# A recurrent-memory and linear-attention kernel on one core: a wider margin for waits on transfers, a new order of all work, and four spinning groups of other tile shapes

## The chip, the core and the metric

The kernel runs on one core of one Trainium2 chip. The time is the device time of that core in microseconds, from one launch of the whole program. A run of it was profiled; the rows of its trace are quoted below as "the profile". Names of the engines in it: PE is TensorE (matmuls), PEld its weight loads, DVE is VectorE, ACT ScalarE, POOL GpSimd, SP SyncE. A `q` behind an engine's name is its instruction queue, which issues transfers.

## What is computed

Two layers of two blocks each over x of 2048 tokens by 512. Block A is an attention with 32 heads of 128 that goes through the tokens in 64 segments of 32, and carries 8 memory rows from one segment to the next, so the segments form one chain. Block B is a linear attention over all tokens with 32 heads of 16.

```python
def A(x, mem0, Wq, Wk, Wv, Wo):
    mem = mem0
    for s in range(64):
        h = concat([mem, x[:, 32*s:32*s+32]], axis=1)        # 8 + 32 rows
        q, k, v = h @ Wq, h @ Wk, h @ Wv                     # 32 heads of 128
        p = softmax(where(mask, q @ k.T * scale, -1e9))
        o = (p @ v) @ Wo
        mem = o[:, :8]
        outs.append(o[:, 8:])
    return concat(outs, axis=1)

def B(x, wqkv, wo):
    pq, pk = phi(q), phi(k)                                  # phi(t) = (t + 1 if t > 0 else exp(t)) + 1e-6
    num, den = pq @ (pk.T @ v), pq @ sum(pk)
    return (num / (den + 1e-6)) @ wo

x = x + A(layernorm(x), ...)
x = x + B(layernorm(x), ...)
x = x + A(layernorm(x), ...)
x = x + B(layernorm(x), ...)
```

## The kernel before

All four large weight matrices are loaded once and stay in SBUF. Tokens are held in 16 tiles of 128 rows; a tile has four segments. A segment is projected to k and q (`kq0`, `kq1`: two halves of the heads) and to v (`v`), each in matmuls that use the PE array as four column groups of 32 (`tile_position`). The results come from PSUM through ScalarE or VectorE (L2009 and L2010, the two branches of one helper `copy`), and are brought into head order by 32x32 transposes of VectorE (L2301). Then, in `mem_attention`, the scores (L2443 for keys of the other groups' tokens, L2435 for the rest), two exponentials on ScalarE, and the new memory rows (L2471); `out_block` (L2563) and `next_mem` (L2593) close the chain to the next segment. `x_attention` (L2501 to L2545) does the same for the segment's 32 tokens, a little later.

The output rows of a segment, in `y_sb`, are brought to their token rows in `dx_sb` by small transfers: `rows_out` issues one 24-row move each on GpSimd's queue (semaphore `dy0`) and on SP's queue (`dz0`) per segment, and for each tile four 8-row moves on either queue (`dy1`, `dz1`). When a tile is complete, one VectorE instruction (L2642) adds `dx_sb` to the tile in `x_sb`. It is the only reader of `dx_sb`. `prepare` normalises the next tile and turns it with a transposing transfer on SP's queue (L2180); `b_in` does block B's first pass over the finished tile, and `b_out` its second pass. Between the layers, `late_queries` does the queries that block B's first pass left out, and GpSimd's queue stores them in DRAM scratch (`pq_scratch`).

No scheduler runs on the chip or in the build. Each piece of work is a node. The table `PLACE` at the top of the file holds one planned number (in ns) for each node, under the key (layer, step, name); a trailing `a` or `v` puts it on ScalarE or VectorE where both can do it. `schedule` sorts all nodes by these numbers; an engine executes its own nodes in that order. `BANKS` gives each PSUM tile its bank. `finalize` (L1765) finds which semaphores a node must wait for, beyond what its engine knows already. A node of ScalarE, VectorE or TensorE with more than one wait keeps the wait whose source is planned last; the others may be put on an earlier node of the same engine, among the last 40, that has no wait yet and is planned later than the source. For a transfer the source's time is taken from the one transfer whose count on the semaphore is the awaited one, as its planned issue plus its planned latency plus a margin (L1808). Several transfers of a group may share a semaphore, and then the wait is over only when all that count towards the value have landed.

At the start, while the weights arrive, TensorE executes groups of matmuls of ones whose results nobody reads (`spin`; L2167 and, without a new weight load, L2139): eleven groups in `first_left_blocks` ahead of the first projections, and six more behind them.

## Time and profile before

| | us |
|---|---|
| three runs: median (lowest to highest) | 1473.34 (1466.6 to 1479.05) |
| the profiled execution, its own time | 1474.65 |
| its span in the trace, first to last instruction | 1472.8 |
| mean granted TensorE clock | 0.997 of full speed |

The page of the profile gives each engine's busy time, the chain of work that ended last, and the costliest groups. Rows of waits read: who waited, for what, the total in us, how often, the longest. Rows of the timeline read: start, length in us, engine, line, what is written and read, count, and in brackets how long the engine had been idle and what ended that. A matmul counts as busy until its result is there, and several overlap; so TensorE can be busy while it does less than it could.

### The profile page before, as it was taken

The numbers are of one execution on the slowest core, as the hardware profiler recorded it, in microseconds if no ns is written. First come the engines' busy times: TensorE is split into PE (matmuls) and PEld (weight loads), VectorE is DVE, ScalarE is ACT, GpSimd is POOL, SyncE is SP. The second block draws the span as 40 slices with busy tenths as digits, with TensorE's granted clock in tenths as the row PEclk, the third lists the DMA queues.
The fourth block names the chain that finished last, engine by engine and source line by source line (L and its number), as shares of the span: only waits on it lengthen the run. The fifth ranks groups of instructions, "written<-read, shape, count | busy, mean of one in ns | idle before, by whom it ended". The sixth has DMA issues, their size and how long they took to land.

```text
span 1472.8 us, 90913 instructions
## 1 busy us (share of the span) xinstructions
PE 1434.8 (97%) x43673; PEld 839.5 (57%) x39641; DVE 1244.9 (85%) x3928; ACT 897.7 (61%) x2532; POOL 205.6 (14%) x407
## 2 busy tenths in 40 slices
PE   9999999999999999999899999999999999999988
PEld 5555555555555555656455555555555565666554
DVE  5888878898887888878888888888888888888878
ACT  3556555656656666665566566556666666666557
POOL 3111111011110101111200110111111111111010
PEclk9999999999999999999999999999999999999999
DMA  9411111111100101112210010111011111101034
GB/s 385 178 50 40 31 29 46 25 26 21 25 25 10 26 20 29 26 22 49 67 25 14 25 29 24 28 26 29 20 23 27 25 28 26 29 14 27 29 65 128
DMA packets 84968, 65.14 MB, mean 44 GB/s; under 512 B 65544, under 2 KB 76360, under 8 KB 83048
## 3 DMA queue, kind: packets, MB, share of 16 engines
q1 hardware_dynamic: 70584, 40.21, 10.2%
q0 software_dynamic: 13840, 18.98, 4.7%
q8 instruction: 326, 5.34, 1.6%
q14 instruction: 58, 0.48, 0.1%
q10 hardware_dynamic: 160, 0.14, 0.0%
HBM read 27.80 MB, written 14.02 MB: 28 GB/s over the span
## 4 chain that ended last, share of the span: by engine, by line
PE 86%; DVE 5%; DMA 5%; ACT 1%; SPq 1%; issue 1%; POOL 1%; DVEq 0%
PE pb L2282 39%; PE pb L2563 18%; PE pb L2139 13%; PE pb L2151 3%; PE pb L2513 3%; DMA dx_sb<-y_sb 2%; PE pb L2755 2%; PE pb L2471 2%; PE pb L2533 2%; PE pb L2435 2%; PE pb L2593 1%; DMA arena_sb<-arena_sb 1%; DVE arena_sb L2488 1%; DMA x_sb<-in_A_x_dram 1%; SPq L2026 1%
## 5 line engine op out<-in xcount | busy, mean ns | idle before, releaser
L2009 ACT ACTIVATE arena_sb<-pb 128x512 bf16<-128x512 f32 (+3 forms) x1013 | 501.4, 524 | 257.5 <-PE pb L2139 108.2
L2282 PE MATMUL pb<-Wk_sb,arena_sb 128*32 128x512 bf16 x4320 | 358.6, 380 | 0.9 <-DVE arena_sb L2010 0.7
L2282 PE MATMUL pb<-Wv_sb,arena_sb 128*32 128x512 bf16 x4608 | 332.6, 380 | 0.0
L2563 PE MATMUL pb<-Wo_sb,arena_sb 128*32 128x256 bf16 x10368 | 323.9, 273 | 0.9 <-DVE arena_sb L2545 0.3
L2301 DVE STREAM_TRANSPOSE arena_sb<-arena_sb 128x256 f32<-128x256 f32 x640 | 259.7, 427 | 35.4 <-ACT arena_sb L2009 25.7
L2563 PEld LDWEIGHTS pb<-Wo_sb,arena_sb 128*32 128x32 bf16 x10368 | 263.9, 97 | 38.8 <-DVE arena_sb L2478 11.7
L2026 POOL DMA_DIRECT2D dx_sb<-y_sb x246 | 125.2, 513 | 997.6 <-DVE y_sb L2575 459.3
L2282 PE MATMUL pb<-Wq_sb,arena_sb 128*32 128x512 bf16 x3088 | 238.0, 380 | 1.1 <-DVE arena_sb L2010 1.1
L2282 PEld LDWEIGHTS pb<-Wk_sb,arena_sb 128*32 128x32 bf16 x4320 | 122.8, 96 | 176.0 <-issue 87.4
L2139 PE MATMUL pb<-Wq_sb,arena_sb 128*32 128x512 bf16 x2032 | 201.4, 379 | 0.0
L2486 ACT ACTIVATE arena_sb<-pb,arena_sb 128x128 bf16<-128x128 f32 x469 | 142.9, 369 | 72.5 <-DVE arena_sb L2540 22.7
L2488 DVE TENSOR_TENSOR arena_sb<-pb,arena_sb 128x128 bf16<-128x128 f32 (+2 forms) x422 | 171.3, 406 | 11.5 <-DMA dx_sb<-y_sb 1.7
L2282 PEld LDWEIGHTS pb<-Wv_sb,arena_sb 128*32 128x32 bf16 x4608 | 114.6, 95 | 70.8 <-issue 7.1
L2010 DVE CAST arena_sb<-pb 128x512 bf16<-128x512 f32 (+2 forms) x248 | 127.4, 516 | 30.9 <-PE pb L2282 8.3
L2009 ACT ACTIVATE outW_sb<-pb 128x256 f32<-128x256 f32 (+1 forms) x132 | 50.7, 384 | 144.0 <-PE pb L2563 96.8
L2282 PEld LDWEIGHTS pb<-Wq_sb,arena_sb 128*32 128x32 bf16 x3088 | 86.0, 97 | 88.1 <-issue 26.3
L2513 PE MATMUL pb<-arena_sb 128*32 128x130 bf16 x3072 | 106.7, 219 | 0.2
L2523 DVE STREAM_TRANSPOSE arena_sb<-arena_sb 128x192 f32<-128x192 f32 x256 | 93.4, 365 | 15.1 <-ACT arena_sb L2486 6.6
L2501 DVE TENSOR_TENSOR arena_sb<-arena_sb,wx_sb 128x1280 bf16<-128x1280 bf16 x128 | 102.1, 797 | 1.2 <-ACT arena_sb L2454 0.8
L2471 PEld LDWEIGHTS pb<-arena_sb 128*32 128x32 bf16 x2016 | 45.5, 96 | 72.0 <-ACT arena_sb L2009 33.9
L2513 PEld LDWEIGHTS pb<-arena_sb 128*32 128x32 bf16 x3072 | 69.2, 96 | 29.8 <-issue 6.5
L2575 DVE TENSOR_TENSOR y_sb<-pb,outW_sb 64x256 bf16<-64x256 f32 x162 | 68.8, 424 | 18.7 <-ACT outW_sb L2009 14.3
(135 smaller groups left out, 1830.2 us busy)
## 6 DMA issues: line engine op xcount, KB each, us to landing
Wk_sb<-in_A_Wk_dram SPq DMA_DIRECT2D x4, 1024.0 KB, 9.6
Wq_sb<-in_A_Wq_dram SPq DMA_DIRECT2D x4, 1024.0 KB, 17.9
Wv_sb<-in_A_Wv_dram SPq DMA_DIRECT2D x4, 1024.0 KB, 25.4
Wo_sb<-in_A_Wo_dram SPq DMA_DIRECT2D x8, 512.0 KB, 22.3
xs_scratch<-x_sb POOLq DMA_DIRECT2D x32, 128.0 KB, 2.7
pq_scratch<-arena_sb POOLq DMA_DIRECT2D x23, 128.0 KB, 2.9
xn_scratch<-arena_sb POOLq DMA_DIRECT2D x20, 128.0 KB, 2.8
lk_scratch<-arena_sb POOLq DMA_DIRECT2D x8, 256.0 KB, 3.3
```

The costliest lines, as they stand in the source:

```text
L2009: return e.activation(o() if callable(o) else o, i() if callable(i) else i, ACTF.Copy)
L2010: return e.tensor_copy(o() if callable(o) else o, i() if callable(i) else i)
L2026: add(eng, lambda e: e.dma_start(o, i), 0.55 if eng == "pool" else 0.66, reads=reads, writes=writes, dsem="%s%d" % (kind, k), lat=lat + (0 ...
L2139: return pe.add_instruction(mybir.InstMatmult(name=nc.get_next_instruction_name(), engine=mybir.EngineType.PE, ins=[pe.lower_ap(x), pe.low ...
L2282: r = pe.matmul(o, blk[:, c, :], w, start=(c == 0), stop=(c == 3), tile_position=(0, 32 * j))
L2301: add("dve", lambda v: v.transpose(dst, src(img[:, k, :].bitcast(F32))), 0.445, reads=[("img", k, h) for h in range(2)], writes=[dkey])
L2486: x = e.activation(o[:, u, :], i()[:, u, :], ACTF.Copy, scale=r[:, u:u + 1])
L2488: return e.tensor_tensor(o, i(), r.unsqueeze(2).to_broadcast([128, n, 128]), ALU.mult)
L2501: add("dve", lambda v: v.tensor_tensor(Px.rearrange("p b (n j x) -> p b n j x", n=20, j=4), PQx[:, r2].rearrange("p b (n x) -> p b n x", n ...
L2513: r = pe.matmul(pv.f32()[32 * i:32 * i + 32, 130 * k:130 * k + 130], cols(b, k, i), vimg[:, r2, 4 * b + i, :], start=True, stop=True, skip ...
L2523: add("dve", lambda v, b=b, k0=k0: v.transpose(oTb[:, s1, b, :, :, k0:k0 + 3].rearrange("p h j k q e -> p k (h j) (q e)").bitcast(F32), ox ...
L2563: r = pe.matmul(tl.f32()[32 * j:32 * j + 32, 0:256], oT[:, b, f, n, :, :, e], Wo_sb[:, 16 * b + 4 * n + 2 * f + e, 256 * d:256 * d + 256], ...
```

## The change

Three edits, and all tables rewritten.

- In `finalize`, the margin added to a transfer's planned landing goes from 200 to 3500 ns. A wait for a transfer is put on an earlier node only if that node is planned more than 3.5 us behind the landing.
- The numbers of `PLACE` and `BANKS` are new: the order on every engine changes in many places, and some nodes change between ScalarE (38 instructions more) and VectorE (16 fewer).
- The first group of spins has seven members instead of eleven; behind them stands `probe`, four groups of matmuls of ones in tiles of 128, 64 and 32 rows by 32 columns, 130 columns long: 12, 24, 24 and 32 matmuls.

```diff
 PLACE = {
...
+    (0, -3, "probe"): "6529 6699 7614 7954",
-    (0, -3, "spin"): "2904 3232 3559 3886 4214 4542 6201 6529 7614 7942 8713",
+    (0, -3, "spin"): "2904 3232 3559 3886 4214 4542 6201",
...
-    (0, 16, "res"): "211182 211998 204479 204698 204916 205364 207357 207576 208346 208564 209014v 209475 210184 212799 210685 210618 212188 211306 211693 209919 216346",
+    (0, 16, "res"): "212152 210540 204448 204666 205430 207394 207612 207831 208275 208494 208944v 209404 212664 211342 210608 212026 211650 209848 210114 212714 217344",
...
-    (0, 17, "ql"): "212310v",
+    (0, 17, "ql"): "207050v",
...
-    (0, 62, "bi"): "670085 670797 671008 671331 671622 672292 672267 677076 677972 678619 679380 680752 681642 681952 681243a 696182 697312 702321 697599 680259 681453 683850 701229",
+    (0, 62, "bi"): "670820 671532 671816 672139 672372 672835 671079 677625 678273 679147 679794 681168 685799 686109 680673a 693078 692364 693404 693079 682870 693590 694228 709495",
...
             if nd.dsem is not None:
-                source[sidx[nd.dsem], nd.dval] = nd.t + 1000 * nd.lat + 200
+                source[sidx[nd.dsem], nd.dval] = nd.t + 1000 * nd.lat + 3500
...
+    def probe(after):
+
+        P.at(0, -3, "probe")
+        shapes = (((1, 4),) * 3, ((2, 4),) * 3, ((1, 4), (2, 4)) * 2, ((4, 4),) * 2)
+        tls = [P.tile() for _ in range(5)]
+        for kinds in shapes:
+
+            def mm(pe, kinds=kinds):
+                x = one_sb[:, 0:65].unsqueeze(1).to_broadcast([128, 2, 65])
+                for rows, cols in kinds:
+                    n = 128 // rows
+                    for k in range(rows):
+                        for j in range(cols):
+                            r = pe.matmul(tls[k if rows > 1 else 4].f32()[32 * j:32 * j + 32, 0:130], one_sb[n * k:n * k + n, 32 * j:32 * j + 32],
+                                          x[n * k:n * k + n], start=True, stop=True, skip_group_check=True, tile_position=(n * k, 32 * j))
+                return r
+            nd = add("pe", mm, c_pe(6, 130), reads=["one"], tiles=tls)
+            nd.order.update(after)
+            after = [nd]
+        return after
...
         def first_left_blocks():
 
-            last = spin(0, -3, "spin", 11, fresh=3)
+            last = probe(spin(0, -3, "spin", 7, fresh=3))
```

In the row `(0, 16, "res")` the entries 0 and 12, 14, 16, 18 are the moves into `dx_sb` on GpSimd's queue, 1 and 13, 15, 17, 19 those on SP's queue, and 20 the addition L2642; `(0, 17, "ql")` is a copy of a segment's queries on VectorE. The last entry of `(0, 62, "bi")` is the store of a tile's queries on GpSimd's queue (`dpq2`). Lines from L2177 on are 22 later in the changed kernel, and one later before that; L2642 is L2664 there, L2443 is L2465.

## The prediction, made before the changed kernel ran

> **What bounds the kernel now.** I read the page first (busy time), then who TensorE waits for, then who VectorE waits for, then stretches of the run, and last one wait in detail. On the page:

> ```profile
> span 1472.8 us, 90913 instructions
> PE 1434.8 (97%) x43673; PEld 839.5 (57%) x39641; DVE 1244.9 (85%) x3928; ACT 897.7 (61%) x2532; POOL 205.6 (14%) x407
> ```

> TensorE sets the time: it is busy in all but 1472.8 - 1434.8 = 38.0 us, and the change adds or removes almost none of its matmuls. What an order can win is in these 38 us and in matmuls that run slowly while counted as busy. The waits of TensorE:

> ```profile
> PE pb L2443 <- DVE arena_sb L2301: 8.5, 5, 2.4
> PE pb L2471 <- DVE arena_sb L2458: 4.8, 3, 1.7
> PE pb L2151 <- DVE x_sb L2642: 1.7, 1, 1.7
> PE pb L2755 <- DMA arena_sb<-xn_scratch: 1.0, 1, 1.0
> PE pb L2755 <- DMA arena_sb<-pq_scratch: 0.9, 1, 0.9
> ```

> The large ones are few and long (five of together 8.5 us, the longest 2.4 us), and VectorE ends them. So the next view is what VectorE itself waited for; these are its rows that end in a transfer:

> ```profile
> DVE arena_sb L2523 <- DMA dx_sb<-y_sb: 5.6, 4, 2.8
> DVE st_sb L2190 <- DMA x_sb<-in_A_x_dram: 5.5, 5, 3.0
> DVE arena_sb L2010 <- DMA dx_sb<-y_sb: 3.6, 4, 2.4
> DVE arena_sb L2842 <- DMA dx_sb<-y_sb: 2.7, 2, 1.7
> DVE arena_sb L2301 <- DMA dx_sb<-y_sb: 2.4, 2, 1.4
> DVE x_sb L2642 <- DMA dx_sb<-y_sb: 1.8, 1, 1.8
> DVE arena_sb L2488 <- DMA dx_sb<-y_sb: 1.7, 1, 1.7
> DVE arena_sb L2540 <- DMA dx_sb<-y_sb: 1.3, 1, 1.3
> DVE arena_sb L2844 <- DMA dx_sb<-y_sb: 0.9, 2, 0.5
> ```

> The eight rows of dx_sb sum to 20.0 us in 17 waits. Only L2642, the residual addition, reads dx_sb. The other 16 waits, 18.2 us, stand at instructions that have no use for the transfer: they were moved there by `finalize`. One of them in full, queue by queue:

> ```profile
> 211.87 3.47 SPq L2026 DMA_DIRECT2D dx_sb<-y_sb  x5
> 216.76 0.23 DVE L2010 COPY arena_sb<-arena_sb 128x256 bf16<-128x256 bf16 x1 [2.42 <-DMA dx_sb<-y_sb]
> 217.40 0.21 PE L2443 MATMUL pb<-arena_sb 128*32 128x64 bf16 x4 [2.01 <-DVE arena_sb L2301]
> 222.30 0.38 DVE L2642 TENSOR_TENSOR x_sb<-x_sb,dx_sb 128x512 bf16<-128x512 bf16 x1
> ```

> SP needs 3.47 us to issue five moves, four of them on one semaphore. The copy waits for all four, stops VectorE for 2.42 us, and behind it in VectorE's queue stand the transposes L2301 that the scores L2443 need: TensorE stops for 2.01 us. The addition that really needs the data runs at 222.30, 5.5 us after the landing.

> The stretches show what this costs in sum (columns: length, then busy time and count of TensorE, its weight loads, VectorE, ScalarE, GpSimd; clock, DMA share, GB/s):

> ```profile
> 60.00:200.00 140.00, 136.56 (x4224) 77.75 (x3864) 120.24 (x395) 84.83 (x243) 18.41 (x35) 1.00 0.18 47
> 200.00:400.00 200.00, 196.29 (x6068) 115.15 (x5516) 170.00 (x553) 119.73 (x352) 28.71 (x55) 0.99 0.14 29
> 400.00:545.00 145.00, 140.49 (x4341) 81.91 (x3892) 122.13 (x396) 86.26 (x249) 18.25 (x35) 0.99 0.09 22
> 545.00:665.00 120.00, 118.87 (x3708) 70.95 (x3360) 100.62 (x329) 78.05 (x236) 17.73 (x34) 1.00 0.11 25
> 705.00:735.00 30.00, 25.83 (x688) 13.66 (x656) 24.76 (x62) 16.53 (x37) 6.75 (x10) 1.00 0.29 69
> 735.00:1000.00 265.00, 259.87 (x7944) 149.02 (x7099) 225.87 (x720) 165.39 (x464) 33.39 (x66) 0.99 0.10 25
> 1000.00:1400.00 400.00, 398.91 (x12360) 238.05 (x11147) 347.08 (x1107) 251.22 (x725) 52.23 (x100) 1.00 0.11 25
> 217.70:221.20 3.50, 3.50 (x70) 1.55 (x56) 2.02 (x8) 2.23 (x7) 0.00 (x0) 0.51 0.02 5
> 838.90:842.40 3.50, 3.50 (x52) 1.13 (x32) 2.14 (x9) 2.55 (x9) 0.00 (x0) 0.51 0.00 0
> ```

> Two stretches are quiet (545 to 665, 1000 to 1400), four are not (60 to 545, 735 to 1000). And after the longest stops TensorE's clock falls to half for about 3.4 us (0.51 in the last two rows; 473.7 to 477.2 is the third). TensorE counts as busy there.

> **The change part by part.** *1. The margin in `finalize`, 200 to 3500.* A wait for a transfer now moves to an earlier instruction only if that one is planned 3.5 us behind the landing. It adds no work. VectorE's rows around the place above, before:

> ```order
> L2301 STREAM_TRANSPOSE arena_sb<-arena_sb 128x256 [waits s_act]
> L2010 COPY arena_sb<-arena_sb 128x16x16 [waits s_dz1]
> L2301 STREAM_TRANSPOSE arena_sb<-arena_sb 128x8x32 [waits s_dve]
> L2301 STREAM_TRANSPOSE arena_sb<-arena_sb 128x256 [waits s_act]
> L2301 STREAM_TRANSPOSE arena_sb<-arena_sb 128x8x32 [waits s_act]
> ...
> L2478 STREAM_TRANSPOSE arena_sb<-arena_sb 128x8x8 [waits s_dve]
> L2642 TENSOR_TENSOR x_sb<-x_sb,dx_sb 128x512 [waits s_dy0,s_dz0,s_dy1]
> ```

> and in the changed kernel at the same addition (now L2664; s_dy and s_dz are the moves into dx_sb by GpSimd's queue and by SP's):

> ```order
> L2562 RECIPROCAL arena_sb<-pb 128x2 [waits s_pe]
> L2545 STREAM_TRANSPOSE arena_sb<-arena_sb 128x3x8x8 [waits s_dy1]
> L2500 STREAM_TRANSPOSE arena_sb<-arena_sb 128x8x8 [waits s_act]
> L2523 TENSOR_TENSOR arena_sb<-arena_sb,wx_sb 128x1280 [waits s_dz0]
> L2664 TENSOR_TENSOR x_sb<-x_sb,dx_sb 128x512 [waits s_dy0,s_dz1]
> ```

> s_dz1 moved from 14 rows ahead of the addition to the addition itself, behind the transposes that feed TensorE; s_dy1 stands three rows ahead. With 5.5 us between landing and addition in the trace, this wait is covered. The flaw of the old margin shows in the diff too: it looks up one of the four moves of a semaphore, and `(0, 16, "res")` puts another of them (212799) behind the waiting copy (`(0, 17, "ql")`, 212310).

> *What these waits cost TensorE*, three ways over the four disturbed stretches (750 us). Idle: 3.44 + 3.71 + 4.51 + 5.13 = 16.8 us, of which the quiet pace (1.13 + 1.09 in 520 us) would leave 3.2: 13.6; plus three spells of half clock, 3.5 x (1 - 0.51) = 1.7 each, 5.1: 18.7 us. Pace: the quiet stretches do (3708 + 12360) / 520 = 30.9 matmuls per us, the disturbed ones 22577 in 750 us, which at 30.9 take 730.6: 19.4 us. VectorE: 20.0, plus 2.5 for the loads of x_sb (5.5 less the 3.0 at the start), less 3.5 at the end (L2642, L2488; below): 19.0. I take 19. The quiet stretches keep 2.2 us idle, of which I count half: 1.

> Were these spells not a consequence of the stops, 5.1 us less would be won: 1456, inside the forecast. I give that 1 in 10, since the clock fell behind the wait of 2.01 us shown above and nowhere in the quiet stretches.

> [...]

> *2. The new order with late landings* moves nearly every row, with the same matmuls. It can only pay where a wait sits at its need already: x_sb loads, and the last addition, where before

> ```profile
> 1415.99 0.56 DVE L2488 TENSOR_TENSOR arena_sb<-pb,arena_sb 128x384 bf16<-128x384 f32 x1 [1.73 <-DMA dx_sb<-y_sb]
> 1411.57 4.39 DMA dx_sb<-y_sb
> 1431.84 4.07 DMA dx_sb<-y_sb
> ```

> moves took 4.39 and 4.07 us to land and cost 1.7 and 1.8 us. Bounds: 0 if these landings stay the critical ones, 3.5 if both are covered; I take 3, since the first stood at an instruction without need. Against it: a new order can leave new gaps of VectorE and ScalarE; the idle shares of the two quiet stretches, 0.3% (1.09 of 400) and 0.9% (1.13 of 120), differ by 0.6%, over the 750 us some 5 us either way; I take 0, as the matmuls and their durations are the same.

> At the layer boundary (705 to 735, 4.2 us idle) ScalarE waited for GpSimd's store of pq:

> ```profile
> 726.74 1.08 ACT L2739 ACTIVATE arena_sb<-pb 128x512 bf16<-128x512 f32 x2 [0.74 <-DMA pq_scratch<-arena_sb]
> ```

> ScalarE's rows there, before:

> ```order
> L2975 ACTIVATE arena_sb<-arena_sb 128x256 [waits s_act] x2
> L2739 ACTIVATE arena_sb<-pb 128x4x128 [waits s_dpq2]
> L2739 ACTIVATE arena_sb<-pb 128x512 [waits s_pe]
> L2987 ACTIVATE arena_sb<-pb,eps_sb 128x512 [waits s_pe]
> L2989 ACTIVATE arena_sb<-arena_sb 128x512 [waits s_act]
> ```

> and now:

> ```order
> L2010 ACTIVATE x_sb<-pb 128x512 [waits s_dve]
> L2761 ACTIVATE arena_sb<-pb 128x4x128
> L2761 ACTIVATE arena_sb<-pb 128x512 [waits s_dpq2]
> L2214 ACTIVATE st_sb<-st_sb,epsb_sb 128x1 [waits s_dve]
> L2216 ACTIVATE st_sb<-st_sb 128x1 [waits s_act]
> ```

> The wait now stands at its need, but the layernorm of the next layer (L2214) is queued right behind. The table issues that store later (709495, was 701229). Nothing (0) to the 1.9 us of TensorE's two waits gained, or 2 us lost; I take 0.

> *3. Four probe groups for four spins.* 48 spin matmuls of 256 columns become 92 of 130, in smaller tiles that no trace row shows. Nearest rows:

> ```profile
> 8.79 0.50 PE L2167 MATMUL pb<-one_sb 128*32 128x256 bf16 x12
> 9.12 1.68 PE L2282 MATMUL pb<-Wk_sb,arena_sb 128*32 128x512 bf16 x28
> 12.51 0.28 PE L2167 MATMUL pb<-one_sb 128*32 128x256 bf16 x1 [1.27 <-issue]
> 1417.75 0.11 PE pb L2471 x8
> ```

> Eight matmuls of 130 columns take 0.11 us, so 92 take 1.3; twelve spins are through in 0.33 us (8.79 to the next start, 9.12), so 48 take 1.3. Equal. Cover: the spins that follow the first Wk work, where TensorE even stood 1.27 us. Without it, at most 1.3 us late; if the smaller tiles let the clock fall once, 1.7. I take 0.

> *Sum*: 19 + 1 + 3 = 23, less 1 for waits that stay in the new places (2 of 17 at the mean of 20.0 / 17 = 1.2, half of it reaching TensorE): 22. The profiled execution took 1474.65 us, 1.3 above the median of the three runs, 1473.34. So 1474.65 - 22 - 1.3 = 1451 us.

> **The rivals.** *A, half is given back.* The waits come back at their needs because landings (up to 4.39) outrun the new distance. For it: L2642 itself waited 1.8 us. Against: once in 32 additions. 11 us saved: 1462; and with the layer boundary 2 us worse and the start 1.7, 1466.

> *B, slower.* The needed additions stop VectorE together with what is now queued behind them, long enough to halve the clock: 2 us of stop and 1.7 us of clock, 3.7 us each. There are 32 additions; above 22 / 3.7 = 6 such stops the gain is gone, and at 12 the time is 1451 + 44 = 1495. Against: that one wait of 1.8 us is the only one at an addition, and 5.5 us of cover at 222.30.

> *C, the change does not do what it says*: the waits find other early places, 1473. Against: the rows of s_dz1 above.

> **How the numbers follow.** Chances: forecast 0.75, A 0.14, B 0.06, C 0.05. About 1% (14.7 us) is what a measurement can tell from no change. The forecast (a gain of 15 to 30) lies on the faster side of 1458.6; A and C within 1%; of B, 0.05 is slower by over 1%, the rest within. Faster 0.75, same 0.20, slower 0.05. Range: below, the bounds in its favour, 22 + 1 (no wait stays) + 0.5 (the end) + 1.9 + 5 = 30.4 off, 1443; above, most of A, 1464. That leaves out B, C and the edge of A.

> **What would show it.** Right: VectorE's rows for dx_sb sum to under 5 us, no spell of half clock after the start, TensorE's wait at L2443 (now L2465) under 2 us in sum, the four disturbed stretches near 30.9 matmuls per us. Wrong: waits of 2 us at L2664; clock of 0.5 between 6 and 20 us; the stretch at the layer boundary more than 2 us longer; a quiet stretch with over 1% idle and no transfer at its end, which would be the new order's own gaps.

## The result and the profile after

| | before | changed |
|---|---|---|
| median (lowest to highest), us | 1472.68 (1466.60 to 1479.05) | 1458.05 (1456.71 to 1459.22) |
| profiled execution, its own time | 1474.65 | 1459.22 |
| its span in the trace | 1472.8 | 1457.5 |

The ratio is 0.990, with a 95% interval of 0.9857 to 0.9943: 14.6 us faster, where 22 were forecast. On the page of the changed kernel:

```profile
span 1457.5 us, 91071 instructions
PE 1433.1 (98%) x43717; PEld 853.0 (59%) x39685; DVE 1231.4 (84%) x3912; ACT 908.4 (62%) x2570; POOL 205.0 (14%) x407
```

TensorE is idle for 1457.5 - 1433.1 = 24.4 us, where it was 38.0. These are all rows of VectorE's waits that end in a transfer, and the longest of TensorE's waits (total in us, how often, the longest):

```profile
DVE st_sb L2212 <- DMA x_sb<-in_A_x_dram: 3.9, 4, 3.0
DVE x_sb L2664 <- DMA dx_sb<-y_sb: 1.1, 2, 0.6
...
PE pb L2260 <- issue: 3.1, 1, 3.1
PE pb L2168 <- POOL one_sb L2084: 2.2, 1, 2.2
PE pb L2152 <- issue: 1.9, 3, 1.3
PE pb L2304 <- DVE arena_sb L2011: 1.8, 7, 0.3
```

The 20.0 us of waits for `dx_sb` have become 1.1, both at the addition itself, and TensorE's wait at the scores (L2465, 8.5 us before) is gone from the list. What is new stands on top: 3.1 us that end in "issue", where TensorE waited for nothing that the profile shows. The stretches (length, then busy time and count of TensorE, its loads, VectorE, ScalarE, GpSimd; clock, DMA share, GB/s), six of those shown of before, then two at the start:

```profile
60.00:200.00 140.00, 136.91 (x4248) 78.97 (x3900) 120.23 (x392) 83.50 (x245) 18.46 (x35) 1.00 0.15 40
200.00:400.00 200.00, 198.31 (x6216) 118.16 (x5648) 170.50 (x567) 124.30 (x361) 28.63 (x56) 1.00 0.12 29
400.00:545.00 145.00, 144.98 (x4521) 90.44 (x4076) 124.73 (x405) 92.80 (x274) 18.24 (x35) 1.00 0.10 22
545.00:665.00 120.00, 119.32 (x3712) 71.63 (x3344) 101.92 (x335) 77.13 (x223) 17.64 (x34) 1.00 0.13 26
735.00:1000.00 265.00, 264.09 (x8144) 158.62 (x7308) 229.39 (x737) 166.43 (x469) 32.73 (x64) 1.00 0.10 23
1000.00:1400.00 400.00, 397.89 (x12352) 236.66 (x11144) 340.15 (x1098) 259.13 (x753) 53.36 (x103) 1.00 0.12 26
...
9.66:13.07 3.41, 0.94 (x21) 0.60 (x24) 1.55 (x4) 0.00 (x0) 2.07 (x11) 1.00 1.02 425
13.07:16.48 3.41, 3.41 (x59) 1.16 (x24) 1.53 (x5) 0.50 (x2) 2.92 (x8) 0.50 1.01 425
```

In the four disturbed stretches TensorE is idle for 3.09 + 1.69 + 0.02 + 0.91 = 5.7 us instead of 16.8, at full clock throughout, and does 23129 matmuls in 750 us, 30.8 per us instead of 30.1. The one spell of half clock is now at the start (13.07 to 16.48). Before, there were three behind 20 us, but by the mean granted clock their number differs between executions: those of the kernel before with a mean of 1.000 took 1466.3 to 1470.8 us, those with 0.997 or less 1470.6 to 1479.1. TensorE's timeline at the start of the changed kernel:

```profile
6.87 0.64 PE L2190 MATMUL pb<-one_sb 128*32 128x130 bf16 x36
7.45 0.41 PE L2229 MATMUL pb<-id_sb,arena_sb 128*32 128x128 bf16 x16
7.68 1.05 PE L2190 MATMUL pb<-one_sb 128*32 128x130 bf16 x56
8.66 0.35 PE L2260 MATMUL pb<-id_sb,arena_sb 128*32 128x128 bf16 x11
12.13 0.27 PE L2260 MATMUL pb<-id_sb,arena_sb 128*32 128x128 bf16 x5 [3.12 <-issue]
12.26 2.43 PE L2304 MATMUL pb<-Wk_sb,arena_sb 128*32 128x512 bf16 x28
```

The stop is in the middle of a group of 16 transposes, and its instructions wait for semaphores only ahead of the first, so no semaphore can be the cause: 11 are done, then nothing happens for 3.12 us. Before, TensorE stopped for 1.27 us in the middle of a group of spins (12.51, shown in the prediction). Counted in the trace, weight loads and semaphore instructions included, both stops are at TensorE's 449th instruction (the first counted as 0), and the later "issue" stops of 0.25 us and more stand a whole multiple of 256 instructions further on (the load or the matmul at that place). The page's row of the queue that brings instructions (packets, MB, share of the transfer engines) fits this:

```profile
q8 instruction: 326, 5.34, 1.5%
```

5.34 MB in 326 packets are 16.4 KB each, and 326 x 256 = 83456 of TensorE's 83591 instructions. The packet that the stops waited for was under way from 10.13 to 11.10 us before and from 9.89 to 10.88 in the changed kernel; TensorE went on at 12.51 and 12.13. So in these traces TensorE's instructions come in blocks of 256, a block is used some 1.3 us after its landing (1.41 and 1.25 here), and a block that TensorE runs through too fast ends in a wait for the next, at what is called a border below. The wait at the 449th instruction took 1.27 us before, 3.12 here and 3.34 in experiment 6.

Where the time went, by stage: how far TensorE's work lies behind the numbers of `PLACE` (start of a matmul in the trace less its planned number, us), at the planned 63, 660, 780 and 1370 us and at the end:

| profiled execution | 63 | 660 | 780 | 1370 | end | planned end |
|---|---|---|---|---|---|---|
| before | -0.5 | 17.2 | 20.4 | 30.8 | 35.8 | 1433.5 |
| changed | 3.7 | 8.4 | 10.9 | 15.6 | 19.6 | 1434.9 |
| margin alone (below) | -0.9 | 4.2 | 7.1 | 10.4 | 14.1 | 1433.5 |

From 63 to 660 and from 780 to 1370 the kernel before lost 17.7 + 10.4 = 28.1 us and the changed one 4.7 + 4.7 = 9.4: 18.7 gained. The end gained 1.0 (5.0 to 4.0), the layer boundary 0.7 (3.2 to 2.5); the start lost 4.2 and the plan is 1.4 longer. Sum: 18.7 + 1.0 + 0.7 - 4.2 - 1.4 = 14.8, where the spans differ by 15.3.

### The profile page after: what moved, and what is told of

It reads as the page before. It is cut to its first block, busy times and chain, and to the rows that moved or that the text cites. A ratio compares the mean times of both kernels' runs of the same rounds, so it can differ in the third digit from the quotient of the medians.

```text
span 1457.5 us, 91071 instructions
## 1 busy us (share of the span) xinstructions
PE 1433.1 (98%) x43717; PEld 853.0 (59%) x39685; DVE 1231.4 (84%) x3912; ACT 908.4 (62%) x2570; POOL 205.0 (14%) x407
## 3 DMA queue, kind: packets, MB, share of 16 engines
q1 hardware_dynamic: 70584, 40.21, 10.7%
q8 instruction: 326, 5.34, 1.5%
## 4 chain that ended last, share of the span: by engine, by line
PE 91%; DVE 5%; ACT 2%; issue 1%; DMA 1%; POOL 0%; DVEq 0%; POOLq 0%; SPq 0%
PE pb L2304 42%; PE pb L2585 19%; PE pb L2140 14%; PE pb L2535 3%; PE pb L2152 3%; PE pb L2777 2%; PE pb L2493 2%; PE pb L2555 2%; PE pb L2457 2%; PE pb L2615 1%; ACT arena_sb L2010 1%; DVE arena_sb L2323 1%; DVE arena_sb L2011 1%; PE pb L2465 1%; DVE arena_sb L2510 0%
## 5 line engine op out<-in xcount | busy, mean ns | idle before, releaser
L2010 ACT ACTIVATE arena_sb<-pb 128x512 bf16<-128x512 f32 (+3 forms) x1011 | 503.4, 528 | 234.1 <-PE pb L2140 114.0
L2323 DVE STREAM_TRANSPOSE arena_sb<-arena_sb 128x256 f32<-128x256 f32 x640 | 260.0, 427 | 36.0 <-ACT arena_sb L2010 28.8
L2508 ACT ACTIVATE arena_sb<-pb,arena_sb 128x128 bf16<-128x128 f32 x516 | 156.9, 367 | 65.4 <-DVE arena_sb L2542 18.0
L2510 DVE TENSOR_TENSOR arena_sb<-pb,arena_sb 128x128 bf16<-128x128 f32 (+2 forms) x397 | 160.9, 406 | 8.8
L2010 ACT ACTIVATE outW_sb<-pb 128x256 f32<-128x256 f32 (+1 forms) x142 | 54.4, 383 | 168.3 <-PE pb L2585 102.5
L2011 DVE CAST arena_sb<-pb 128x512 bf16<-128x512 f32 (+2 forms) x254 | 125.0, 497 | 33.0 <-PE pb L2140 11.5
L2545 DVE STREAM_TRANSPOSE arena_sb<-arena_sb 128x192 f32<-128x192 f32 x256 | 93.3, 364 | 12.1 <-ACT arena_sb L2508 9.6
L2523 DVE TENSOR_TENSOR arena_sb<-arena_sb,wx_sb 128x1280 bf16<-128x1280 bf16 x128 | 101.9, 796 | 1.3 <-ACT arena_sb L2476 0.8
L2535 PEld LDWEIGHTS pb<-arena_sb 128*32 128x32 bf16 x3072 | 70.5, 96 | 31.5 <-issue 8.0
L2597 DVE TENSOR_TENSOR y_sb<-pb,outW_sb 64x256 bf16<-64x256 f32 x162 | 68.7, 424 | 23.0 <-ACT outW_sb L2010 18.2
L2493 PEld LDWEIGHTS pb<-arena_sb 128*32 128x32 bf16 x2016 | 47.2, 95 | 61.6 <-ACT arena_sb L2010 35.6
```

Source lines behind the costliest of these rows:

```text
L2010: return e.activation(o() if callable(o) else o, i() if callable(i) else i, ACTF.Copy)
L2011: return e.tensor_copy(o() if callable(o) else o, i() if callable(i) else i)
L2323: add("dve", lambda v: v.transpose(dst, src(img[:, k, :].bitcast(F32))), 0.445, reads=[("img", k, h) for h in range(2)], writes=[dkey])
L2508: x = e.activation(o[:, u, :], i()[:, u, :], ACTF.Copy, scale=r[:, u:u + 1])
L2510: return e.tensor_tensor(o, i(), r.unsqueeze(2).to_broadcast([128, n, 128]), ALU.mult)
L2523: add("dve", lambda v: v.tensor_tensor(Px.rearrange("p b (n j x) -> p b n j x", n=20, j=4), PQx[:, r2].rearrange("p b (n x) -> p b n x", n ...
```

## The experiments

The first theory was that of the prediction for the margin, with the blocks of instructions for what was missing. Ratios are to the kernel before on the same chip, with 95% intervals.

**1. The margin alone.** The kernel before with one number changed.

```diff
-                source[sidx[nd.dsem], nd.dval] = nd.t + 1000 * nd.lat + 200
+                source[sidx[nd.dsem], nd.dval] = nd.t + 1000 * nd.lat + 3500
```

> The kernel before with only the margin at 3500. Theory: the rule carries the gain. VectorE's waits for dx_sb fall from 20.0 us to under 3, no spell of half clock behind 20 us, and the start keeps its one stop of 1.3 us at 12.5 us. Some stops of 0.3 to 1 us stay or come at every 256th instruction of TensorE (4.8 us of them before). Time 1456 us (1452 to 1460), 16 us under before. Rival, the new order carries half of it: the waits move to other instructions of the old order and 8 to 12 us of them are left, 1464 us or more.

Measured: 1454.24 us (1453.48 to 1454.75), ratio 0.9874 [0.9848, 0.9900]. The waits for `dx_sb` on VectorE are one, at the last addition, and no clock spell follows the start:

```profile
DVE st_sb L2190 <- DMA x_sb<-in_A_x_dram: 3.8, 4, 3.0
DVE x_sb L2642 <- DMA dx_sb<-y_sb: 2.4, 1, 2.4
```

The margin carries all of the gain and more: the changed kernel is slower than this (experiment 4).

**2. The new order with the old margin.** The changed kernel with 200 in that line.

> The changed kernel with the margin back at 200: the new order and the probe groups alone. Theory: VectorE's waits for dx_sb are back at 12 to 20 us, with 1 to 3 spells of half clock behind the longest stops of TensorE, and the start has the stop of 3.1 us as in the changed kernel: 1473 us (1468 to 1478), no gain over before. Rival, the new order covers late landings by itself: waits for dx_sb under 6 us, 1462 us or less.

Measured: 1471.25 us (1470.36 to 1473.94), ratio 0.9994 [0.9981, 1.0007]. VectorE waits again at instructions without need, such as the copy (L2011) and the transposes (L2323):

```profile
DVE arena_sb L2011 <- DMA dx_sb<-y_sb: 5.5, 4, 3.3
...
DVE arena_sb L2510 <- DMA dx_sb<-y_sb: 1.3, 2, 0.9
DVE arena_sb L2354 <- DMA dx_sb<-y_sb: 1.2, 1, 1.2
DVE arena_sb L2545 <- DMA dx_sb<-y_sb: 1.2, 2, 1.0
DVE arena_sb L2323 <- DMA dx_sb<-y_sb: 1.0, 2, 0.6
```

In all there are 11.6 us of such waits, 13 in number, where the kernel before had 20.0 us in 17. The new order does not cover late landings by itself, but the two parts overlap: from 63 to 660 and 780 to 1370 us this execution loses 7.3 + 10.6 = 17.9 us against `PLACE`, less than the 28.1 of before, and on this chip, where the kernel before took 1471.76, the margin is worth 1471.76 - 1454.24 = 17.5 us in the old order and 1471.25 - 1459.07 (experiment 4) = 12.2 in the new one. One thing was missed: there was no spell of half clock after the start, although one copy held VectorE for 3.3 us and TensorE for as long. Experiment 12 shows why.

**3. The lookup mended instead of the margin.** The kernel before, margin 200, a transfer's time being the latest of all that count towards the value.

```diff
+        far = {}
+        for (si, v), t in sorted(source.items()):
+            if si >= len(ENGINES):
+                far[si] = source[si, v] = max(far.get(si, 0), t)
```

> The kernel before with the margin at 200, but a transfer's time in the table of sources is the latest of all transfers that count towards the awaited value (36 waits move, against 96 with the margin of 3500). Theory, the lookup of one of several moves is the flaw: every wait for dx_sb of over 0.5 us in the trace of before goes except the two at the last tiles (1.7 and 1.8 us), and the time is within 3 us of the margin alone. Rival, the planned latency is the flaw (2.0 to 2.4 us planned, 3.9 to 5.3 measured at the waits): waits of 1 to 2.5 us come back at other instructions, 8 us of them or more, 1464 us.

Measured: 1456.87 us (1455.94 to 1458.66), ratio 0.9896 [0.9865, 0.9927]; 4.3 us of waits for `dx_sb` are left. So 36 moved waits do most of what the margin does (2.6 us less): the main flaw was the lookup of one of several moves, and the margin of 3500 hides it, with some of the too short planned latencies.

**4. The changed kernel again**, on the same chip as 1 to 3.

> The changed kernel once more, beside the others on one chip: 1458 us, with the stop of 3.1 us at about 12 us and the half clock behind it, if these belong to the kernel and not to one execution. If they belong to the one execution, neither shows and the time is 1454.

Measured: 1459.07 us (1458.80 to 1461.07), 4.8 us over the margin alone, with no overlap of the two. The stop at the 449th instruction lasted 2.9 us and the half clock followed (12.56 to 15.98): they belong to the kernel. Order and probe groups together cost some 5 us.

**5 to 7. The probe groups.** Each is the changed kernel with other matmuls of ones. 5: four groups of twelve matmuls of 256 columns, in tiles of 128 by 32 (88 instructions fewer, loads included).

```diff
-        shapes = (((1, 4),) * 3, ((2, 4),) * 3, ((1, 4), (2, 4)) * 2, ((4, 4),) * 2)
-        for kinds in shapes:
+        for i in range(4):
...
+                x = one_sb[:, 0:128].unsqueeze(1).to_broadcast([128, 2, 128])
+                for u in range(3):
+                    for j in range(4):
+                        r = pe.matmul(tls[i].f32()[32 * j:32 * j + 32, 0:256], one_sb[:, 32 * j:32 * j + 32], x,
+                                      start=True, stop=True, skip_group_check=True, tile_position=(0, 32 * j))
```

> The changed kernel with four spinning groups of 12 matmuls of 256 columns, in tiles of 128 by 32, in place of the four probe groups (48 matmuls for 92). Theory, TensorE's instructions come in blocks of 256 and the third block is there only at 12.1 to 12.5 us: a stop again at the 449th instruction, ending at 12.3 to 12.6 us, but of 1.2 to 1.5 us, since fewer instructions lie ahead of the first work; no half clock behind it; 3.5 us less than the changed kernel, 1454.5. Rival, the tile shapes let the clock fall: the stop stays near 3 us, only the clock recovers, 1456.

6: the probe's 92 matmuls of 130 columns, all in tiles of 128 by 32.

```diff
-        shapes = (((1, 4),) * 3, ((2, 4),) * 3, ((1, 4), (2, 4)) * 2, ((4, 4),) * 2)
+        for rounds in (3, 6, 6, 8):
...
+                for k in range(rounds):
+                    for j in range(4):
+                        r = pe.matmul(tls[k % 5].f32()[32 * j:32 * j + 32, 0:130], one_sb[:, 32 * j:32 * j + 32], x,
+                                      start=True, stop=True, skip_group_check=True, tile_position=(0, 32 * j))
```

> The changed kernel with 92 matmuls of 130 columns in the four groups as in the probe, but all in tiles of 128 by 32. Theory of blocks: the number of instructions decides, not the shape of the tiles: the stop of about 3.1 us ending at 12.1 us and the spell of half clock as in the changed kernel, 1458. Rival, the smaller tiles are the cause: a stop of 1.5 us or less, no half clock, 1454.5.

7: experiment 5 with all spins as one matmul of 512 and one of 256 columns in place of three of 256.

```diff
-                x = one_sb[:, 0:128].unsqueeze(1).to_broadcast([128, 2, 128])
-                for u in range(3):
+                for u in range(2):
+                    x = one_sb[:, 0:128].unsqueeze(1).to_broadcast([128, 4 - 2 * u, 128])
```

> The changed kernel with every spinning group at the start of one 512-column and one 256-column matmul for each group of columns in place of three of 256 (8 matmuls for 12), the four probe groups too. The same columns in fewer instructions. Theory of blocks: 256 instructions then last longer than the 5.6 to 6.0 us that the next block took, so the stop at the 449th instruction is under 0.5 us, and the first work is done before it: 4 us less than the changed kernel, 1454, or a little less than with the spins of 256. Rival, the stop belongs to a wait for the weights that the instruction counts do not touch: a stop of 1.3 us or more ending at 12.1 to 12.5 us.

The stop at that instruction, in the timelines of 5 and of 6:

```profile
12.51 0.28 PE L2168 MATMUL pb<-one_sb 128*32 128x256 bf16 x1 [0.38 <-issue]
```

```profile
12.39 0.27 PE L2257 MATMUL pb<-id_sb,arena_sb 128*32 128x128 bf16 x5 [3.34 <-issue]
```

In 5 the stop is shorter than the 1.2 to 1.5 us expected, since a wait for VectorE of 0.92 us just before had taken up the time. With the fewest instructions (7) no stop is there (TensorE waits 1.3 us for VectorE at 11.4 us instead). So the count of instructions sets the stop, and the shape of the tiles does not: narrow matmuls in full tiles gave the same 3.34 us. But the time did not follow: 1460.03 us (5; ratio 0.9901 [0.9877, 0.9925]), 1458.35 (6; 0.9897 [0.9869, 0.9924]) and 1460.95 (7; 0.9908 [0.9885, 0.9931]), where 5 and 7 should have been 4 us under the changed kernel. And the profiled execution of 6 had no half clock behind its long stop (its granted clock is 1.000, that of two others 0.999 and 0.998). Both theories had missed something. In the stages, 5 has won back the start (-0.2 at 63, where the changed kernel has 3.7), and lost it again on the way: 13.1 us from 63 to 660 and 780 to 1370, instead of 9.4. The stops of 0.25 us and more at the block borders after 20 us (from the start of one instruction to that of the next) sum to 16.8 us in 5, against 11.2 and 11.0 in the two profiles of the changed kernel.

**8 to 11. Where the borders lie.** Second theory: taking 88 instructions out of the start moves the border of every later block against the work, and the kernel before has its borders in good places. On the margin alone: 8 repeats it; 9 makes its eleven first groups wide (88 instructions fewer); 10 does the same and adds 88 in the six groups behind the first weights, so that all later borders are back. 11 is experiment 5 with the same 88 more behind the first weights. The edit of 10 in `spin` (the first eleven groups are those with `fresh` of 3; 9 has `(2, 2, 2)` for `(1,) * 6` and `fresh` for the last bracket):

```diff
-                x = one_sb[:, 0:128].unsqueeze(1).to_broadcast([128, 2, 128])
-                for u in range(3):
+                wide = fresh > 1
+                for u, k in enumerate((4, 2) if wide else (1,) * 6):
+                    x = one_sb[:, 0:128].unsqueeze(1).to_broadcast([128, k, 128]) if k > 1 else one_sb[:, 0:128]
...
-                        if u < fresh:
+                        if u < (fresh if fresh > 1 else (2 if i < 4 else 1)):
```

> The margin alone once more, as the partner of the next two: 1454 us (1453 to 1456), a stop of 0 to 1.3 us at TensorE's 449th instruction, and beyond 20 us 4 to 7 us of stops of 0.25 us and more at every 256th.

> The margin alone, with the eleven first spinning groups as one matmul of 512 and one of 256 columns for each group of columns (88 instructions of TensorE fewer, the same columns): all later work lies 88 instructions earlier against the blocks of 256. Theory, the place of the block borders in the work decides: no stop at the 449th instruction (1.2 us won), but the stops at later borders grow from 5 to 8 to 11 us, so 1456 to 1458 us, 2 to 4 more than the margin alone. Rival, the new order of work itself makes its stops and the borders of the old order are harmless wherever they lie: 1453 us, later stops still 4 to 6 us.

> As the kernel with 88 instructions fewer, and the six spinning groups behind the first weights get 88 instructions more (matmuls of 128 columns, the same columns), so that all later work lies against the blocks as in the margin alone. Theory: no stop at the 449th instruction or one under 0.5 us, later stops 4 to 7 us as before: 1453 us, 0.5 to 1.5 under the margin alone. Rival, fewer instructions at the start cost elsewhere, whatever the borders: 1456 us or more, as the kernel with 88 fewer.

> The changed kernel with spins of 256 columns for the probe groups (88 instructions fewer) and 88 more in the six spinning groups behind the first weights, so that the borders of the blocks lie behind the start as in the changed kernel. Theory: the stop of 3.1 us and the half clock go (3.5 to 4.5 us), and the later stops stay at 9 to 11 us, where the same spins without the 88 had 16.8: 1454.5 us. Rival, a start without the stop is given back later whatever the borders: 1458 to 1460, as with the spins alone.

| kernel | its profiled execution: stops at borders after 20 us, number and sum | its own time | median time (ratio, interval) |
|---|---|---|---|
| 1, margin alone | 8, 4.9 us | 1453.48 | 1454.24 |
| 8, margin alone again | 12, 7.9 | 1454.98 | 1453.87 (0.9872 [0.9848, 0.9895]) |
| 9, 88 instructions fewer | 25, 17.2 | 1462.33 | 1461.62 (0.9926 [0.9904, 0.9948]) |
| 10, and 88 more behind | 11, 6.5 | 1453.53 | 1456.87 (0.9891 [0.9868, 0.9914]) |
| changed; again | 19, 11.2; 19, 11.0 | 1459.22; 1461.07 | 1458.05; 1459.07 |
| 5, 88 fewer | 26, 16.8 | 1460.50 | 1460.03 |
| 11, and 88 more behind | 18, 10.9 | 1458.62 | 1458.31 (0.9904 [0.9878, 0.9929]) |
| 6, borders as in the changed | 14, 8.7 | 1456.27 | 1458.35 |

The sums do what the second theory says, in both orders: 88 fewer make them grow, 88 more behind bring them back. With the borders in the same places they still differ by up to 3 us from one execution to another (1 and 8, 6 and the changed kernel); the steps from 8 to 9 (9.3 us) and from 9 to 10 (10.7) are clear of that. Kernel 9 does the same work as 8 in the same order, with 88 instructions fewer, and takes 1461.62 - 1453.87 = 7.8 us longer, more than the 2 to 4 expected. TensorE's waits in 9 show it; all "issue" rows of this view sum to 10.7 us there, and to 3.5 (1) and 6.0 (8) in the margin alone:

```profile
PE pb L2151 <- issue: 2.9, 1, 2.9
PE pb L2514 <- issue: 2.5, 4, 0.8
PE pb L2594 <- issue: 2.2, 4, 0.7
...
PE pb L2564 <- issue: 1.8, 3, 0.7
```

The median times of 10 and 11 miss: both are some 4 us over what was expected. In both, a stop at the start remains, since the added instructions run through their own block too fast; in 11 it is 1.98 us, at 18.45 us. In 10:

```profile
13.37 0.23 PE L2168 MATMUL pb<-one_sb 128*32 128x128 bf16 x1 [1.46 <-issue]
```

For 10 this does not explain the miss: with this stop its profiled execution took 1453.53 us, as expected. Its five others took 1455.68 to 1458.71, without a trace, so what made them longer stays open, and the rival's "1456 us or more" (fewer instructions at the start cost elsewhere) is not ruled out for some 3 us. Of the 7.8 us of kernel 9, putting the borders back returned 1461.62 - 1456.87 = 4.8 in the median. That the start's loss can be had back without moving the rest is therefore not shown.

**12. Graded stops.** Two things were open: what a wait at the addition would cost (rival B), and when the clock falls. On the margin alone, VectorE executes extra statistics instructions ahead of 30 additions.

```diff
+                for i in range(2 + G % 6 if n == 128 else 0):
+                    add("dve", lambda v, i=i: v.bn_stats(st_sb[:, 0, 10:16], dx_sb[:, G % 2, :]), c_dve(512), reads=parts, writes=["junk"])
```

> The margin alone, with VectorE held up at 30 of the 32 residual additions by 2 to 7 extra statistics instructions ahead of it (0.7 us each, results read by nobody): stops of VectorE of 1.4, 2.1, 2.8, 3.5, 4.2 and 4.9 us, five of each. What a wait at the addition would cost: theory, TensorE stops for the same time less about 0.8 us, 70 us in sum, and half clock for 1.7 us each behind some 12 of them, 1544 us (1500 to 1560). Rival, work ahead in the queues covers the addition: under 40 us in sum, 1500 or less. On the clock: theory of a grid, the clock changes only at whole multiples of 3.413 us from its first rise, and falls where TensorE was idle for 2.0 us or more of the interval that ends there: no fall behind intervals with under 1.8 us idle, a fall behind nearly all with over 2.1, and some single stops of 2.1 to 3.4 us that lie across a border are followed by none. Rival, the length of one stop decides: every stop over 2.1 us is followed by a fall and none under 1.9.

Measured: 1558.87 us, one run. (Their numbers in `PLACE` put them ahead of the addition, though the code adds them behind it. The lengths came six times each for the three shorter and four times for the three longer stops, 126 instructions, 86.9 us.) TensorE is idle for 72 us more than in the margin alone (96.0 against 23.8) and spends 16 spells at half clock. The 16 spells are 19 intervals of 1.7 us lost each; with the 72 us that makes 104 of the 104.6 us over experiment 1, 3.5 for each addition. So a stop at the addition goes to TensorE nearly whole (72 of 86.9 us), and rival B's price of 2 us and 1.7 of clock was about right; only the waits were not there.

The clock: in this profile every change lies a whole multiple of 3.4133 us behind the first rise (up to 454 of them, none off by more than 0.02 us), and the same holds in the other thirteen profiles of the study; in the kernel before, the falls at 217.75, 473.75 and 838.97 us lie 62, 137 and 244 such intervals behind the rise at 6.12. What counts here is TensorE's idle time within one such interval. Two stops, and the intervals around them (TensorE's busy time is the first number with a count; the clock is the third from the end):

```profile
929.30 0.40 PE L2282 MATMUL pb<-Wq_sb,arena_sb 128*32 128x512 bf16 x4 [2.34 <-DVE arena_sb L2010]
...
1023.77 0.30 PE L2471 MATMUL pb<-arena_sb 128*32 128x130 bf16 x8 [4.00 <-DVE arena_sb L2458]
```

```profile
926.22:929.63 3.41, 1.07 (x52) 0.54 (x36) 3.24 (x8) 0.44 (x3) 0.00 (x0) 1.00 0.00 0
929.63:933.04 3.41, 3.41 (x44) 0.83 (x25) 2.46 (x9) 0.97 (x3) 1.08 (x2) 0.50 0.34 84
1018.38:1021.79 3.41, 1.39 (x44) 0.42 (x28) 3.24 (x6) 1.57 (x6) 0.00 (x0) 1.00 0.02 5
1021.79:1025.20 3.41, 1.43 (x48) 0.82 (x44) 3.31 (x13) 0.00 (x1) 0.00 (x0) 1.00 0.00 0
1025.20:1028.62 3.42, 3.42 (x136) 2.40 (x117) 3.05 (x9) 1.84 (x7) 0.49 (x1) 1.00 0.02 5
```

A stop of 2.34 us that lies within one interval is followed by half clock for the next; a stop of 4.00 us, cut by the end of an interval into 2.02 and 1.98, by none. Of the intervals at full clock, all 16 with 2.21 us idle or more were followed by a fall, and none with 2.02 or less. Three of the 16 spells went on for a second interval: TensorE had been idle for 0.86 to 1.34 us of the first, and for 0.81 or less in the 13 others, so at half clock 0.86 us was enough to keep it there. The theory of the grid holds and that of the length of a stop falls. It also explains the misses above: the stop of 3.3 us in experiment 2 (1.43 and 1.87 on the two sides) and that of 3.34 us in 6 (1.32 and 2.02).

## Why the prediction came out as it did

- **The margin (19 + 1 us).** Right in mechanism and size: 18.7 us gained between the start, the boundary and the end, and experiment 1 gets there with the margin alone (8.4 us lost in these stretches, where the changed kernel loses 9.4). Inside it, the 1 us for the quiet stretches failed: their idle time went from 2.2 to 2.8 us (0.68 + 2.11), 1.1 of it in stops at block borders (0.7 before), the rest mostly in short waits for VectorE and ScalarE. The three spells of half clock are gone, as counted; that they come from stops held, but by the share of an interval, not by the length of a stop.
- **"The flaw of the old margin" in the lookup** was right, by experiment 3.
- **The end (3 us).** Mis-sized: 1.0. The wait at L2488 went, that at the last addition shrank from 1.8 to 0.6, but the stops at borders in the last 50 us grew from 2.5 us (0.53, 1.03 and 0.98 between starts) to 3.4 (1.11, 1.63 and 0.70), and TensorE waits 1.1 us for VectorE at L2763, a wait that before has no row for.
- **The layer boundary (0, between -2 and 1.9)**: 0.7 gained. **New gaps of the order (0, within 5)**: its plan ends 1.4 us later, and from 63 to 660 and 780 to 1370 it loses 9.4 us where the margin alone loses 8.4.
- **The probe groups: the step that failed.** The prediction counted only columns ("Eight matmuls of 130 columns take 0.11 us, so 92 take 1.3; twelve spins are through in 0.33 us, so 48 take 1.3. Equal.") and took 0, at most 1.7. The columns were right: the chain of waits counts 0.47 and 0.88 us for the probe, 1.35. But 88 more instructions bring TensorE to the 449th at 9.01 us instead of 11.24, and the block is usable only at 12.1 (12.5 before): 1.8 us more of stop and a spell of half clock (1.7), 3.5 of the 4.2 us at 63; for the other 0.7 no row was found. The prediction's bounds of 1.3 or 1.7 us missed that the two prices come together. The row of 1.27 us "issue" that the prediction took for cover was this wait itself.
- **The residual of 1 us**: right, 1.1 us of waits are left.

The forecast of 1451 was 7 us low: 4.2 of the start, 2 at the end, 1.4 of the plan, less 0.7 at the boundary. That 1458 lies inside the range of 1443 to 1464 is in part luck: its upper end was drawn for waits that come back, and what used it up is the start. The time alone lies nearer to rival A's 1462 than to 1451; the waits tell the two apart. Rival A falls, with only 1.1 us of waits at the additions, and so does C, since the waits did not find other early places. B's mechanism exists at its price, but its waits did not come. Of the signs named, the waits for `dx_sb`, the scores (L2465) and the pace came as right ones, and the clock of 0.5 between 6 and 20 us as a wrong one.

The fastest version is the margin alone in the old order: 1454.24 and 1453.87 us in two sets, ratio 0.9872 [0.9848, 0.9895] in the second.

## What to carry to other kernels

A wait that is moved ahead of its need must look at the last transfer that counts towards it, not at one of them; a planner's error there stops an engine for work that doesn't need the data (VectorE 16 times here, for 18.2 us). Where TensorE runs through near 60 instructions per us (256 in 4.3 us here), count instructions as well as columns: filler made of many small matmuls brings the next wait for instructions forward (from 11.24 to 9.01 us here, by 88 instructions), and any edit at the start moves all later borders (88 instructions fewer made experiment 9 take 7.8 us longer), so that a few us of difference between two orders can be the place of the borders and not the orders. To tell the two apart, add or take away filler of a known count and see whether the stops follow.
